# Attention scores of the later chunks: full-width products of stacked K parts, one head at a time

## The chip, the cores and the metric

One core of one Trainium2 chip runs the whole program. The metric is the device time of one execution in microseconds (us), the median of the runs of one measurement; lower is better.

## What is computed

Sliding-window attention with a few sink keys over q, k, v of shape 4 x 8 x 768 x 64 (batch, heads, positions, head size), and behind it a gated feed-forward block on the 3072 resulting rows of 512:

```python
scores = (1 / sqrt(D)) * q @ k.T
keep = (pos < n_sink) | ((0 <= rel) & (rel < window))      # 4 sinks, window 128
a = softmax(where(keep, scores, -1e9))                      # row by row, sum + 1e-9
x = (a @ v).transpose(0, 2, 1, 3).reshape(3072, 512)
out = (x @ w_a * (x @ w_b)) @ w_out                         # d_ff = 1536
```

All inputs are fp32. A product of two fp32 matrices is made from rounded parts: `h` (high, type fp32r) and `l` (the rest), as high*high + high*low + low*high.

## The kernel before, in words

The 24 tiles of 128 query rows are dealt into chunks. The first four tiles (tile 0 of each batch) have a path of their own (`first_tiles`). Then `run` takes the chunks of `CHUNKS` in turn: the feed-forward block (`moe`) of one chunk runs on TensorE, and between its products the attention of the next chunk is slipped in (`between`, a generator that is advanced by some steps at each of 33 places). Chunk 0 (2 tiles) uses `parts_exact`, plain fp32; chunks 1 to 6 (3 tiles each, the last two from two batches) use `parts_split`, and these are the later chunks that the change touches.

`moe` walks over j = 0..11: twelve products for `a` (4 blocks of 128 x 3 rounded pairs, 384 columns wide for three tiles), twelve for `b`, and nine of 512 columns into the outputs `o0`, `o1`, `o2` for the j before. ScalarE copies `a` to `g`, VectorE multiplies by `b`, ScalarE rounds it to `gh`, and GpSimd (j < 10) makes the rest `gl`.

`parts_split` of one chunk works on pairs of heads m = 0..3 (8 heads). `prepare(m)` loads K and q of both heads stacked on 128 partitions (head 2m on 0 to 63, head 2m+1 on 64 to 127), and GpSimd rounds them and makes the rests (`round` L383, `rest` L386): `kh`, `kl`, `qh`, `ql`. `scores(m, i)` for tile i makes six products of 64 partitions and 264 columns (128 keys before, 8 sink columns, 128 own keys), three for each head, on the upper and the lower half of TensorE's rows, into two PSUM banks, `s` for the even head and `av` for the odd one. One such group of six is called a unit below; there are 6 chunks x 4 pairs x 3 tiles = 72. VectorE merges the window (L611), subtracts the mask and takes the row minimum (L612), ScalarE makes the exponentials with their sums (L615), VectorE the reciprocal (L617, L618) for both heads in one instruction, ScalarE scales (L620) and copies the 8 sink columns (L625). Later `transposes(h)` turns the three tiles of one head into bank `t` (L631), VectorE writes them to `pt` (L633), `av(m)` multiplies with v (L642: 64 weight columns for each head, so the two heads use the left and the right half of TensorE's columns; called AV below), `sinks_t` and `sinks_av` (L651, L662) add the sinks.

Each PSUM tag (`s`, `av`, `t`, `a`, `b`, `o0`, `o1`, `o2`) is one bank with one buffer. The pool `io` has 6 buffers for everything that is loaded in this phase. The order of instructions on each engine is fixed when the program is built: the framework's scheduler places them, starting from the order of the code.

Of the kernel before, what the change touches and what calls it, by code (L numbers as in the profile page):

```python
# [19 lines left out]
P = 128  # L20
# [207 lines left out]
class Fast:  # L228
    def __init__(self, tc, ctx, ident, ins, out, chk):
        self.tc, self.nc, self.ident, self.out, self.chk = tc, tc.nc, ident, out, chk  # L230
        self.kT, self.kD, self.qT, self.qP, self.vB, self.vS, self.kq0, self.v0, self.wa, self.wb, self.wo = ins
# [5 lines left out]
        self.at = pool("f_at", 4)  # L237
# [159 lines left out]
    def prep_kq(self, places, m, tag):  # L397
        raws = []
        for b, t0, n, s0, nb, kw, *_ in places:
            kr = self.io([P, 4 * KB - NS], F32, f"kr{tag}_{m}_{b}")  # L400
            self.nc.sync.dma_start(kr[:, :kw], self.kT[b, m, :, s0 * KB:s0 * KB + kw])
            raws.append(kr)
        qr = self.io([P, 3 * P], F32, f"qr{tag}_{m}")
        for b, t0, n, *_, i in places:
            self.nc.sync.dma_start(qr[:, i * P:(i + n) * P], self.qP[b, m, :, t0 * P:(t0 + n) * P])
        kh, kl = (self.sp.tile([P, MK], F32R, tag=k, name=f"{k}{tag}_{m}") for k in ("kh", "kl"))
        qh, ql = (self.sp.tile([P, 3 * P], F32R, tag=k, name=f"{k}{tag}_{m}") for k in ("qh", "ql"))
        for kr, (*_, kw, col, _, _) in zip(raws, places):
            cols = slice(col, col + kw)
            self.round(kh[:, cols], kr[:, :kw])  # L410
            self.rest(kl[:, cols], kr[:, :kw], kh[:, cols])
# [133 lines left out]
    def attention(self, parts, xf, after):  # L545

        prepare, values, sinks, scores, transposes, av, sinks_t, sinks_av = parts
        values(0)
        for k in range(6 * NP + 7):
            m, r = divmod(k, 6)  # L550
            if r == 2 and m:
                transposes(2 * m - 1)
            if r % 2 == 0 and m < NP:
                scores(m, r // 2)
            if r == 0 and m > 1 and m % 2:
                sinks_av(m // 2 - 1, 1, xf)
            if r == 0 and m + 1 < NP:
                prepare(m + 1)
            if r == 1 and m:
                transposes(2 * m - 2)  # L560
            if r == 3 and m and m % 2 == 0:
                sinks_t(m // 2 - 1)
            if r == 4 and m:
                av(m - 1, xf)
                if m < NP:
                    values(m)
# [489 lines left out]
```

## Time and profile before

| | |
|---|---|
| median of 3 runs | 780.69 us (779.58 to 780.88) |
| profiled execution, its own time | 778.73 us |
| span of its instructions | 777.0 us |
| TensorE matmul busy | 766.9 us (99%) |
| VectorE, ScalarE, GpSimd busy | 370.9, 372.2, 191.2 us |
| granted TensorE clock, mean | 0.999 |

The profiled execution is 1.96 us faster than the median of the timed runs; 1.7 us of its time lie outside the span. Matmul records overlap, since a matmul's record reaches from its start to the modelled landing of its result while the next one already streams; so "99% busy" says that TensorE never has nothing under way, and what a matmul costs is read from start to start.

### The profile page before, as it was taken

Reading aid. Unit: us, or ns where it says so; the run is one execution under the profiler, and the core shown is the slowest. Engines: PE = TensorE matmul, PEld = TensorE weight load, DVE = VectorE, ACT = ScalarE, POOL = GpSimd, SP = SyncE. Lnnn points to the kernel's source line nnn. Section 1 sums busy time; section 2 is a strip of 40 time slices with the busy share of each in tenths; the row PEclk is TensorE's granted clock in tenths of the full one; section 3 lists DMA queues with packets and bytes.
Section 4 is the critical chain, followed back from the end, with each engine's and each line's share of the span. In section 5 each row is a group of like instructions: output and inputs, shape, how many; then the busy total and the mean of one; then the engine's idle time right before and its main releaser. Section 6 shows DMA issues by size and latency. Waiting matters only on the chain.

```text
span 777.0 us, 12872 instructions
## 1 busy us (share of the span) xinstructions
PE 766.9 (99%) x4580; PEld 661.9 (85%) x4582; DVE 370.9 (48%) x1161; ACT 372.2 (48%) x1123; POOL 191.2 (25%) x252
## 2 busy tenths in 40 slices
PE   8999999999999999999999999999999999999997
PEld 6887777888888889888888888888888888899996
DVE  6899999345344443345433444334443445221001
ACT  6577755465355553555435554354544555331111
POOL 2300022043214132231413314134241432101110
PEclk9999999999999999999999999999999999999999
DMA  8996101312102142132321223213343130010001
GB/s 336 398 346 222 33 26 27 130 39 77 55 28 80 60 152 93 41 99 67 127 91 62 80 89 118 78 68 100 97 131 99 59 93 19 18 41 1 1 1 43
DMA packets 44261, 72.36 MB, mean 93 GB/s; under 512 B 4576, under 2 KB 24096, under 8 KB 44192
## 3 DMA queue, kind: packets, MB, share of 16 engines
q1 hardware_dynamic: 41024, 65.98, 25.9%
q10 hardware_dynamic: 3168, 5.51, 1.9%
q8 instruction: 37, 0.61, 0.3%
q14 instruction: 32, 0.26, 0.1%
HBM read 65.18 MB, written 6.29 MB: 92 GB/s over the span
## 4 chain that ended last, share of the span: by engine, by line
PE 94%; DMA 2%; DVE 2%; ACT 1%; SPq 0%; issue 0%
PE b L829 27%; PE a L829 26%; PE o L857 26%; PE s L605 5%; PE av L642 4%; PE t L631 2%; DMA kx<-in_kD_dram 1%; DMA v<-in_v_dram 1%; PE s L715 1%; PE sk L662 1%; PE skt L651 1%; PE t L740 0%; PE afirst L829 0%; PE t L752 0%; PE av L605 0%; PE av L506 0%
## 5 line engine op out<-in xcount | busy, mean ns | idle before, releaser
L829 PE MATMUL b<-xh,w_b 128*128 128x384 f32 (+2 forms) x768 | 215.2, 344 | 0.0
L829 PE MATMUL a<-xh,w_a 128*128 128x384 f32 (+2 forms) x760 | 214.5, 346 | 0.0
L857 PE MATMUL o<-w_o,gh 128*128 128x512 f32 x576 | 184.1, 401 | 0.0
L878 POOL TENSOR_TENSOR gl<-g,gh 128x384 fp32r<-128x384 f32 (+1 forms) x70 | 68.1, 973 | 359.0 <-ACT gh L876 358.8
L829 PEld LDWEIGHTS a<-xh,w_a 128*128 128x128 f32 x760 | 137.5, 188 | 11.9 <-ACT p L615 2.1
L829 PEld LDWEIGHTS b<-xh,w_b 128*128 128x128 f32 x768 | 139.4, 188 | 7.6
L829 PE MATMUL b<-xl,w_b 128*128 128x384 f32 (+2 forms) x384 | 130.1, 339 | 0.0
L829 PE MATMUL a<-xl,w_a 128*128 128x384 f32 (+2 forms) x380 | 128.2, 337 | 0.0
L857 PEld LDWEIGHTS o<-w_o,gh 128*128 128x128 f32 x576 | 104.4, 188 | 20.1 <-ACT p L615 1.0
L873 DVE TENSOR_TENSOR g<-b,g 128x384 f32<-128x384 f32 (+2 forms) x96 | 53.4, 557 | 140.2 <-PE b L829 134.8
L857 PE MATMUL o<-w_o,gl 128*128 128x512 f32 x288 | 113.6, 395 | 0.0
L615 ACT ACTIVATE p<-p,st 128x136 f32<-128x136 f32 x144 | 57.7, 402 | 83.2 <-DVE st L612 80.8
L867 ACT COPY g<-a 128x384 f32<-128x384 f32 (+2 forms) x95 | 45.1, 475 | 106.9 <-PE a L829 101.6
L876 ACT CAST gh<-g 128x384 fp32r<-128x384 f32 (+2 forms) x96 | 49.2, 512 | 97.6 <-DVE g L873 96.7
L829 PEld LDWEIGHTS a<-xl,w_a 128*128 128x128 f32 x380 | 71.5, 188 | 3.0
L829 PEld LDWEIGHTS b<-xl,w_b 128*128 128x128 f32 x384 | 72.3, 188 | 1.9
L857 PEld LDWEIGHTS o<-w_o,gl 128*128 128x128 f32 x288 | 54.1, 188 | 13.4 <-DVE gl L878 0.8
L633 DVE TENSOR_TENSOR pt<-t,tri 128x768 f32<-128x768 f32 x48 | 45.8, 955 | 38.1 <-PE t L631 38.1
L611 DVE COPY_PREDICATED s<-own,s 128x128 f32<-128x128 uint16 x72 | 21.1, 293 | 87.4 <-PE av L605 75.7
L620 ACT ACTIVATE p<-p,st 128x136 f32<-128x136 f32 x144 | 51.0, 402 | 23.0 <-DVE st L618 21.0
L617 DVE TENSOR_SCALAR st<-st 128x2 f32<-128x2 f32 x72 | 14.9, 207 | 49.6 <-ACT p L615 49.6
L386 POOL TENSOR_TENSOR kl<-kr,kh 128x536 fp32r<-128x536 f32 (+2 forms) x32 | 36.7, 1146 | 1.8
(174 smaller groups left out, 1046.0 us busy)
## 6 DMA issues: line engine op xcount, KB each, us to landing
raw_a<-in_wa_dram SPq DMA_DIRECT2D x12, 512.0 KB, 7.8
raw_b<-in_wb_dram SPq DMA_DIRECT2D x12, 512.0 KB, 7.3
raw_o<-in_wo_dram SPq DMA_DIRECT2D x12, 512.0 KB, 7.0
chk_a<-in_wa_dram SPq DMA_DIRECT2D x24, 256.0 KB, 3.0
chk_b<-in_wb_dram SPq DMA_DIRECT2D x24, 256.0 KB, 2.9
chk_o<-in_wo_dram SPq DMA_DIRECT2D x24, 256.0 KB, 2.9
out_dram<-os ACTq DMA_DIRECT2D x21, 256.0 KB, 2.1
kr<-in_kT_dram SPq DMA_DIRECT2D x16, 268.0 KB, 2.8
```

The costliest lines, as they stand in the source:

```text
L386: self.nc.gpsimd.tensor_tensor(o, i, high.bitcast(F32), op=ALU.subtract)
L605: nc.tensor.matmul(ss[e], lhsT=q[half[e], cols], rhs=k[half[e], c0:c0 + SW], start=n == 0, stop=n == 2)
L615: nc.scalar.activation(p[:, e], p[:, e], AF.Exp, bias=st[:, 0, e:e + 1], scale=-1.0, accum_out=st[:, 1, e:e + 1])
L620: nc.scalar.mul(p[:, e], p[:, e], st[:, 3, e:e + 1])
L633: nc.vector.tensor_tensor(self.pt_pair()[:, e].rearrange("p (c m) q -> p c m q", m=2), tp.unsqueeze(2).to_broadcast(shape), self.tri.unsqu ...
L642: nc.tensor.matmul(ps[half[e], c * P:(c + ns) * P], lhsT=v[:, e, blk, :], rhs=pt[:, e, sl:sl + ns, :], start=j == 0, stop=j == len(groups) ...
L829: mm = self.nc.tensor.matmul(ps[:, cols], lhsT=w[:, ksl], rhs=x[:, kk, cols], start=start and kk == 0 and i == 0, stop=kk == NK - 1 and i ...
L857: nc.tensor.matmul(outs[i], lhsT=g[:, sl], rhs=w, start=j == 0 and k == 0, stop=j == NJ - 1 and k == 2)
L867: nc.scalar.copy(g[:, :n], pa[:, :n])
L873: nc.vector.tensor_tensor(g[:, :n], pb[:, :n], g[:, :n], op=ALU.mult)
L876: nc.scalar.copy(gh[:, :n], g[:, :n])
L878: e.tensor_tensor(gl[:, :n], g[:, :n], gh[:, :n].bitcast(F32), op=ALU.subtract)
```

## The change

In `parts_split` the heads are taken one at a time. `prepare(h)` loads q of one head twice (partitions 0 to 63 and again 64 to 127; the host lays q out so already) and K of a pair only for even heads. GpSimd writes one tile `ks` of 128 partitions that holds the high part of the head's K on one half and the rest on the other. `scores(h, i)` is then two products over all 128 partitions: `ks` by `qh`, and `ks` by `ql`, into bank `s` alone. The softmax steps are issued for one head. Bank `av` now takes the results of `av` and `sinks_av`. The steps of a chunk are 30 instead of 31, with a new order; `p` and `st` have 6 buffers instead of 4, `v` has 2 instead of 1. AV and the joined key blocks (`groups`) are as before.

```diff
-        self.at = pool("f_at", 4)
+        self.at = pool("f_at", 6)
...
+    def halves(self, h):
+        return (slice(0, D), slice(D, P)) if h % 2 == 0 else (slice(D, P), slice(0, D))
+
+    def prep_kq(self, places, h, tag):
+        if h % 2 == 0:
+            self.kr = []
+            for b, t0, n, s0, nb, kw, *_ in places:
+                kr = self.io([P, 4 * KB - NS], F32, f"kr{tag}_{h}_{b}")
+                self.nc.sync.dma_start(kr[:, :kw], self.kT[b, h // 2, :, s0 * KB:s0 * KB + kw])
+                self.kr.append(kr)
+        qr = self.io([P, 3 * P], F32, f"qr{tag}_{h}")
         for b, t0, n, *_, i in places:
-            self.nc.sync.dma_start(qr[:, i * P:(i + n) * P], self.qP[b, m, :, t0 * P:(t0 + n) * P])
...
+            self.nc.sync.dma_start(qr[:, i * P:(i + n) * P], self.qT[b, h, :, t0 * P:(t0 + n) * P])
+        ks = self.sp.tile([P, MK], F32R, tag="kh", name=f"ks{tag}_{h}")
+        qh, ql = (self.sp.tile([P, 3 * P], F32R, tag=k, name=f"{k}{tag}_{h}") for k in ("qh", "ql"))
+        kh, kl = self.halves(h)
+        for kr, (*_, kw, col, _, _) in zip(self.kr, places):
+            kr = kr[(h % 2) * D:(h % 2 + 1) * D, :kw]
+            self.round(ks[kh, col:col + kw], kr)
+            self.rest(ks[kl, col:col + kw], kr, ks[kh, col:col + kw])
         self.round(qh, qr)
         self.rest(ql, qr, qh)
-        return kh, kl, qh, ql
+        return ks, qh, ql
...
-        v = self.sp.tile([P, 2, MB, D], F32, tag="v", name=f"v{tag}_{m}", bufs=1)
+        v = self.sp.tile([P, 2, MB, D], F32, tag="v", name=f"v{tag}_{m}")
...
+        for h in range(H + 2):
+            for i in range(3):
+                if h < H:
+                    scores(h, i)
+                if i == 0:
+                    if h % 2 == 1 and h > 2:
+                        av(h // 2 - 1, xf)
+                    if h + 1 < H:
+                        prepare(h + 1)
+                    elif h + 1 == H and after:
+                        after[0](0)
+                    if h < H and h % 2 == 0:
+                        values(h // 2)
+                    if h % 4 == 3:
+                        sinks(h // 4)
+                elif h > 4 and h % 4 == 1:
+                    sinks_av(h // 4 - 1, i - 1, xf)
+                if i == 1 and 1 <= h <= H:
+                    transposes(h - 1)
+                if i == 2 and h and h % 4 == 0:
+                    sinks_t(h // 4 - 1)
+                yield
...
+        def scores(h, i):
+            ks, qh, ql = kq[h]
+            u = f"{tag}_{h}_{i}"
+            ps = self.ps.tile([P, SW], F32, tag="s", name=f"s{u}")
+            for n, q in enumerate((qh, ql)):
+                nc.tensor.matmul(ps, lhsT=q[:, i * P:(i + 1) * P], rhs=ks[:, c0s[i]:c0s[i] + SW],
+                                 start=n == 0, stop=n == 1)
+            p = self.at.tile([P, SW], F32, tag="p", name=f"p{u}")[:, :W]
+            st = self.at.tile([P, 4], F32, tag="st", name=f"st{u}")
             mask = self.m1 if tiles[i] == 1 else self.mg
...
-            ps = self.ps.tile([P, nt * P], F32, tag="t", name=f"av{tag}_{m}")
+            ps = self.ps.tile([P, nt * P], F32, tag="av", name=f"av{tag}_{m}")
...
-            ps = self.ps.tile([P, n], F32, tag="t", name=f"sk{tag}_{g}_{pr}")
+            ps = self.ps.tile([P, n], F32, tag="av", name=f"sk{tag}_{g}_{pr}")
...
-                steps = 6 * NP + 7 if c else H * len(nrows) + 5
+                steps = 30 if c else H * len(nrows) + 5
```

The order on TensorE, in the chunk of batch 1 (names begin with its number; the numbers behind are the pair or head, the tile and the buffer), where the AV of the first pair stands. Before, from the last product of `b` of one j to the first of `o`:

```order
L829 MATMUL b_3_2890<-xh,w_b_743 128x384
L605 MATMUL s_1_1_2_2908<-kh_1_1_2645,qh_1_1_2647 128x264
L605 MATMUL av_1_1_2_2909<-kh_1_1_2645,qh_1_1_2647 128x264
L605 MATMUL s_1_1_2_2908<-kl_1_1_2646,qh_1_1_2647 128x264
L605 MATMUL av_1_1_2_2909<-kl_1_1_2646,qh_1_1_2647 128x264
L605 MATMUL s_1_1_2_2908<-kh_1_1_2645,ql_1_1_2648 128x264
L605 MATMUL av_1_1_2_2909<-kh_1_1_2645,ql_1_1_2648 128x264
L642 MATMUL av_1_0_2929<-pt,v_1_0_2617 64x256 x4
L642 MATMUL av_1_0_2929<-pt,v_1_0_2617 64x128 x4
L857 MATMUL o_0_2599<-w_o_765,gh_2_2823 128x512 x2
```

and with the change:

```order
L822 MATMUL a_3_2952<-xh,w_a_698 128x384
L604 MATMUL s_1_3_0_2967<-ks_1_3_2879,qh_1_3_2880 128x264
L604 MATMUL s_1_3_0_2967<-ks_1_3_2879,ql_1_3_2881 128x264
L635 MATMUL av_1_0_2979<-pt,v_1_0_2706 64x256 x4
L635 MATMUL av_1_0_2979<-pt,v_1_0_2706 64x128 x4
L822 MATMUL b_3_3004<-xh,w_b_743 128x384
```

A unit of six half-height products has become a group of two of full height, and AV stands behind such a group.

The place on TensorE where two groups of scores stand closest, at the start of the same chunk. Before, tile 2 of pair 0 stood between `b` and `o`:

```order
L829 MATMUL b_1_2708<-xh,w_b_513 128x384
L605 MATMUL s_1_0_2_2726<-kh_1_0_2393,qh_1_0_2395 128x264
L605 MATMUL av_1_0_2_2727<-kh_1_0_2393,qh_1_0_2395 128x264
L605 MATMUL s_1_0_2_2726<-kl_1_0_2394,qh_1_0_2395 128x264
L605 MATMUL av_1_0_2_2727<-kl_1_0_2394,qh_1_0_2395 128x264
L605 MATMUL s_1_0_2_2726<-kh_1_0_2393,ql_1_0_2396 128x264
L605 MATMUL av_1_0_2_2727<-kh_1_0_2393,ql_1_0_2396 128x264
L857 MATMUL o_0_2599<-w_o_555,gh_0_2667 128x512 x2
```

With the change the groups of head 0, tile 2 and of head 1, tile 0 stand around five products of `a`:

```order
L822 MATMUL a_1_2752<-xh,w_a_487 128x384 x2
L604 MATMUL s_1_0_2_2739<-ks_1_0_2418,qh_1_0_2419 128x264
L604 MATMUL s_1_0_2_2739<-ks_1_0_2418,ql_1_0_2420 128x264
L822 MATMUL a_1_2752<-xl,w_a_487 128x384
L822 MATMUL a_1_2752<-xh,w_a_487 128x384 x2
L822 MATMUL a_1_2752<-xl,w_a_487 128x384
L822 MATMUL a_1_2752<-xh,w_a_487 128x384
L604 MATMUL s_1_1_0_2767<-ks_1_1_2699,qh_1_1_2700 128x264
L604 MATMUL s_1_1_0_2767<-ks_1_1_2699,ql_1_1_2701 128x264
```

Both write bank `s`, so the second group waits until VectorE has read the first; between the two groups ahead of them lie seven products of `a`, and nine or more of `moe` or an AV between any others of this chunk.

The order on GpSimd for the preparation of one pair before:

```order
L383 TENSOR_SCALAR kh_1_3_3003<-kr_1_3_1_2999 128x536
L386 TENSOR_TENSOR kl_1_3_3004<-kr_1_3_1_2999,kh_1_3_3003 128x536
L383 TENSOR_SCALAR qh_1_3_3005<-qr_1_3_3001 128x384
L386 TENSOR_TENSOR ql_1_3_3006<-qr_1_3_3001,qh_1_3_3005 128x384
L878 TENSOR_TENSOR gl_4_3026<-g_4_2975,gh_4_3025 128x384
L878 TENSOR_TENSOR gl_5_3115<-g_5_3091,gh_5_3114 128x384
```

and of two heads now:

```order
L383 TENSOR_SCALAR qh_1_2_2784<-qr_1_2_2781 128x384
L383 TENSOR_SCALAR ks_1_2_2783<-kr_1_2_1_2779 64x536
L386 TENSOR_TENSOR ql_1_2_2785<-qr_1_2_2781,qh_1_2_2784 128x384
L386 TENSOR_TENSOR ks_1_2_2783<-kr_1_2_1_2779,ks_1_2_2783 64x536
L871 TENSOR_TENSOR gl_1_2805<-g_1_2765,gh_1_2804 128x384
L383 TENSOR_SCALAR qh_1_3_2880<-qr_1_3_2877 128x384
L383 TENSOR_SCALAR ks_1_3_2879<-kr_1_2_1_2779 64x536
L386 TENSOR_TENSOR ql_1_3_2881<-qr_1_3_2877,qh_1_3_2880 128x384
L386 TENSOR_TENSOR ks_1_3_2879<-kr_1_2_1_2779,ks_1_3_2879 64x536
L871 TENSOR_TENSOR gl_2_2903<-g_2_2863,gh_2_2902 128x384
```

The four instructions now stand once for each head, with as many columns as before (K on 64 partitions instead of 128), and one `gl` of `moe` between two heads.

## Rows read from the trace of the kernel before

**Rows 1.** The page: busy time of each engine with its share of the span and its instructions, and the chain of work that ended last, by engine.

```profile
PE 766.9 (99%) x4580; PEld 661.9 (85%) x4582; DVE 370.9 (48%) x1161; ACT 372.2 (48%) x1123; POOL 191.2 (25%) x252
...
PE 94%; DMA 2%; DVE 2%; ACT 1%; SPq 0%; issue 0%
```

**Rows 2.** Timeline of PE around one unit between `a` and `b`: start us, duration us, engine, line, operation, tiles, shapes. The odd head's products (`av`) start with the even head's and are left out.

```profile
252.23 0.34 PE L829 MATMUL a<-xh,w_a 128*128 128x384 f32 x1
252.50 0.39 PE L605 MATMUL s<-kh,qh 64*128 64x264 f32 x1
...
252.73 0.28 PE L605 MATMUL s<-kl,qh 64*128 64x264 f32 x1
...
252.85 0.28 PE L605 MATMUL s<-kh,ql 64*128 64x264 f32 x1
...
253.06 0.44 PE L829 MATMUL b<-xh,w_b 128*128 128x384 f32 x1
253.35 0.34 PE L829 MATMUL b<-xl,w_b 128*128 128x384 f32 x1
```

**Rows 3.** Timeline of PE: transposes without a unit behind them (255.28), products of `o`, and transposes with a unit behind them (257.70).

```profile
255.28 0.49 PE L631 MATMUL t<-ident,p 128*128 128x128 f32 x3
255.53 0.70 PE L857 MATMUL o<-w_o,gh 128*128 128x512 f32 x2
256.06 0.40 PE L857 MATMUL o<-w_o,gl 128*128 128x512 f32 x1
256.30 0.63 PE L857 MATMUL o<-w_o,gh 128*128 128x512 f32 x2
...
257.70 0.49 PE L631 MATMUL t<-ident,p 128*128 128x128 f32 x3
258.12 0.38 PE L605 MATMUL s<-kh,qh 64*128 64x264 f32 x1
...
258.68 0.45 PE L829 MATMUL a<-xh,w_a 128*128 128x384 f32 x1
258.96 0.34 PE L829 MATMUL a<-xl,w_a 128*128 128x384 f32 x1
```

**Rows 4.** Timeline of PE: one full-height product of `sinks_av` (L662) between `a` and `b`, then the first and the last of twelve products of `b`, 384 columns each.

```profile
269.57 0.34 PE L829 MATMUL a<-xh,w_a 128*128 128x384 f32 x1
269.75 0.34 PE L662 MATMUL sk<-xh,xl 128*128 128x384 f32 x1
269.93 0.34 PE L829 MATMUL b<-xh,w_b 128*128 128x384 f32 x1
...
271.86 0.34 PE L829 MATMUL b<-xh,w_b 128*128 128x384 f32 x1
```

**Rows 5.** Timeline of PE: the first and the last of twelve products of `a`, 256 columns each, in the feed-forward of the chunk with two tiles.

```profile
172.37 0.28 PE L829 MATMUL a<-xh,w_a 128*128 128x256 f32 x1
...
173.69 0.28 PE L829 MATMUL a<-xh,w_a 128*128 128x256 f32 x1
```

**Rows 6.** Timeline of PE: products of 128 columns, the first and the tenth of a run.

```profile
30.89 0.28 PE L829 MATMUL afirst<-xl,w_a 128*128 128x128 f32 x1
...
31.90 0.28 PE L829 MATMUL afirst<-xl,w_a 128*128 128x128 f32 x1
```

**Rows 7.** Timeline of PE: an AV with no unit ahead of it, between `o` and `a` (256 columns wide).

```profile
208.32 0.40 PE L857 MATMUL o<-w_o,gl 128*128 128x512 f32 x1
208.65 1.52 PE L642 MATMUL av<-pt,v 128*64 128x256 f32 x16
210.10 0.39 PE L829 MATMUL a<-xh,w_a 128*128 128x256 f32 x1
210.33 0.29 PE L829 MATMUL a<-xl,w_a 128*128 128x256 f32 x1
```

**Rows 8.** The full-height scores of chunk 0 (L715), from the answer on that line: the waits that stand ahead of them in the queue of PE (PEldq); duration in ns, min/median/max, first and last start.

```profile
L715 PEldq EVENT_SEMAPHORE  x7: 51/51/51, 31.5 to 102.4; - x7
```

**Rows 9.** Timeline of PE at the last of these waits (102.4).

```profile
102.62 0.40 PE L829 MATMUL b<-xh,w_b 128*128 128x512 f32 x1
...
102.85 0.61 PE L715 MATMUL s<-kx,qx 128*128 128x264 f32 x2
```

**Rows 10.** Timeline of DVE and ACT behind one unit whose last products are in the first row.

```profile
336.32 0.28 PE L605 MATMUL s<-kh,ql 64*128 64x264 f32 x1
...
336.95 0.28 DVE L611 COPY_PREDICATED s<-own,s 128x128 f32<-128x128 uint16 x1
...
337.34 0.29 DVE L612 CUSTOM_DVE_ANT_0 p<-s,mg 128x136 f32<-128x136 f32 x1
...
339.38 0.71 ACT L620 ACTIVATE p<-p,st 128x136 f32<-128x136 f32 x2
```

**Rows 11.** Groups by line, GpSimd, shapes kept apart: count, busy us, mean ns of one, idle time before them and what ended it.

```profile
L878 POOL TENSOR_TENSOR gl<-g,gh 128x384 fp32r<-128x384 f32 x60 | 60.8, 1013 | 324.1 <-ACT gh L876 324.0
L386 POOL TENSOR_TENSOR ql<-qr,qh 128x384 fp32r<-128x384 f32 x24 | 25.0, 1044 | 1.1
L386 POOL TENSOR_TENSOR kl<-kr,kh 128x536 fp32r<-128x536 f32 x16 | 22.2, 1387 | 0.8
L383 POOL TENSOR_SCALAR qh<-qr 128x384 fp32r<-128x384 f32 x24 | 13.1, 546 | 27.4 <-PE av L605 22.6 <-DMA qr<-in_qP_dram 4.6
L383 POOL TENSOR_SCALAR kh<-kr 128x536 fp32r<-128x536 f32 x16 | 10.2, 639 | 28.7 <-DMA kr<-in_kT_dram 17.5 <-issue 11.0
```

More of the change, by code (lines that the diff above doesn't have):

```diff
@@ L547, in attention @@
         prepare, values, sinks, scores, transposes, av, sinks_t, sinks_av = parts
[L548 to L566, printed above, removed]
-                if m % 2:
-                    sinks(m // 2)
-            if r == 5 and m and m % 2 == 0:
-                sinks_av(m // 2 - 1, 0, xf)
-            if r == 5 and m == NP - 1 and after:
-                after[0](0)
-            yield
+        for h in range(H + 2):
[20 more added lines that the diff above has]
+                yield
     def parts_split(self, segs):
@@ L587, in parts_split, with prepare @@
         half = (slice(0, D), slice(D, P))
[L589 to L590 removed]
+        def prepare(h):
+            kq[h] = self.prep_kq(places, h, tag)
         def values(m):
@@ new lines, in scores @@
+        def scores(h, i):
[7 more added lines that the diff above has]
+            st = self.at.tile([P, 4], F32, tag="st", name=f"st{u}")
+            mask = self.m1 if tiles[i] == 1 else self.mg
+            nc.vector.copy_predicated(ps[:, :P], self.own.bitcast(mybir.dt.uint16), ps[:, W:])
+            nc.vector.tensor_tensor_reduce(out=p, in0=ps[:, :W], in1=mask[:, :W], scale=-0.125, scalar=BIG,
+                                           op0=ALU.add, op1=ALU.min, accum_out=st[:, 0:1])
+            nc.scalar.activation(p, p, AF.Exp, bias=st[:, 0:1], scale=-1.0, accum_out=st[:, 1:2])
+            nc.vector.tensor_scalar(st[:, 2:3], st[:, 1:2], 1e-9, None, op0=ALU.add)
+            nc.vector.reciprocal(st[:, 3:4], st[:, 2:3])
+            nc.scalar.mul(p, p, st[:, 3:4])
+            state[h, i] = p
+            if h % 4 == 0:
+                sc[h // 4, i] = self.at.tile([P, 4, NS], F32, tag=f"sc{i}", name=f"sc{u}", bufs=2)
+            nc.scalar.copy(sc[h // 4, i][:, h % 4, :], p[:, P:])
@@ L695, in do_prep @@
             if h % 2 == 0:
-                v = self.sp.tile([P, 2, MB, D], F32, tag="kl", name=f"vx{u}")
+                v = self.sp.tile([P, 2, MB, D], F32, tag="v", name=f"vx{u}")
                 nc.sync.dma_start(v[:, :, :nb], self.vB[b, h // 2, :, :, s0:s0 + nb])
@@ L977, in run, with body @@
         return val, self.ok
-def body(tc, kT, kD, qT, qP, vB, vS, kq0, v0, wa, wb, wo, nw, out):
+def body(tc, kT, kD, qT, vB, vS, kq0, v0, wa, wb, wo, nw, out):
     nc = tc.nc
@@ L988, in body @@
         with ExitStack() as ctx:
-            f = Fast(tc, ctx, ident, (kT, kD, qT, qP, vB, vS, kq0, v0, wa, wb, wo), out, chk)
+            f = Fast(tc, ctx, ident, (kT, kD, qT, vB, vS, kq0, v0, wa, wb, wo), out, chk)
             val, ok = f.run(lambda: scalars_to_float(tc, cp, raw), lambda val, gp: verdict(tc, cp, ident, chk, val, gp))
```

52 lines of the change are left out of this document (4 added, 48 removed).

## The prediction

> **What bounds the kernel now.** First the page: TensorE has work in 99% of the span, every other engine in less than half, and the chain that ended last is TensorE's own for 94% [rows 1]. So the kernel ends when TensorE has streamed everything in its queue, and an edit is worth what it changes between the starts of TensorE's matmuls. The second view is therefore the timeline of PE, read from start to start. A plain product of 384 columns costs 0.1755 us (eleven steps from 269.93 to 271.86, 1.93 us) [rows 4], one of 256 columns 0.120 us (eleven steps from 172.37 to 173.69) [rows 5], one of 512 columns 0.233 us (six steps from 256.30 to 257.70) [rows 3]. Against these a unit of scores can be priced, borders included.
>
> **What a unit costs today.** Between the last product of `a` (252.23) and the second of `b` (253.35) lie 1.12 us [rows 2]; two plain products would take 0.351 us, so the unit costs 0.769 us. It has three parts: 0.27 us from the last `a` to the unit, where 0.1755 is plain (0.095 us of entry); 0.56 us inside; and 0.29 us from the first to the second `b` (0.115 us of exit). The six products run two by two, one on each half of the rows, so the inside holds only three steps. The last two start 0.12 us apart (252.73, 252.85) [rows 2]; the rest is again border. Behind transposes the price is the same: without a unit they cost 0.25 us and the two products behind them 0.53 instead of 0.466 us; with a unit 0.42 us until its start, 0.56 us inside and 0.28 us to the second `a` [rows 3]. The difference is 0.42 + 0.56 + 0.28 - 0.1755 - 0.25 - 0.064 = 0.77 us.
>
> An AV with no unit ahead has an entry of its own: 0.33 us from the last `o` to AV where 0.233 is plain, and 0.23 us behind it where 0.120 is plain [rows 7]. So leaving for work on half the array, and coming back, costs about 0.1 us each way. The order of before puts an AV directly behind the third tile of pairs 1 to 3, that is behind 18 of the 72 units. There the unit has no exit, and AV no entry.
>
> The Trainium skill says as much in "TensorEngine Tiling (Array Packing)", section Key Properties: changing the tiling mode, not just the tile, drains TensorE. The trace agrees, with 0.095 us in and 0.11 us out.
>
> **What the change removes.** 54 units with both borders at 0.769 us are 41.5 us. The 18 ahead of an AV have an entry and 0.56 us, 0.655 us, but their AVs then pay 0.10 us themselves: 18 x 0.555 = 10.0 us. The first unit of all stands in two pieces among the products of `b`, which adds one visit more, 0.77 us. Together 52.3 us.
>
> **What it adds on TensorE.** 6 chunks x 8 heads x 3 tiles x 2 = 288 full-height products of 264 columns. No row shows such a product in fp32r. It is nearest to the 256-column product; 8 columns more at the slope between 256 and 512 columns, (0.233 - 0.120) / 256 us each, give 0.1235 us, and 288 of them 35.6 us. From below, 128 columns still take 0.112 us (nine steps from 30.89 to 31.90 [rows 6]), so less than 32.3 us is excluded; from above, the row of 384 columns would make 50.5 us. I take 0.1235: 264 is next to 256. Borders I take as nothing: the full-height product of `sinks_av` between `a` and `b` starts 0.18 us behind one neighbour and 0.18 us ahead of the next, plain spacing for 384 columns, although its operands come from other engines [rows 4]. A wait of its own in the queue costs nothing either where it is met in time: at 102.4 one stands ahead of a full-height score, which starts 0.23 us behind a 512-column product, as if there were no wait [rows 8, 9].
>
> The sum: 52.3 - 35.6 = 16.7 us less. AV, its column halves, the transposes and the feed-forward keep their counts. The profiled execution would go from 778.73 to 762.0 us; the median stands 1.96 us above that execution, so I predict 780.69 - 16.7 = **764.0 us**.
>
> **What lies beside.** GpSimd prepares each head with the four instructions that served a pair. Their columns are the same, so between half and all of the old time for the K part; I take all: 0.546 + 0.639 + 1.044 + 1.387 = 3.62 us a head [rows 11], and twice the old sum of GpSimd's preparation in all, some 90 us more on 191 [rows 1]. Where does it wait? `ks` has two buffers, so head h+1 may start when tile 2 of head h-1 is through TensorE, and must be done before tile 0 of head h+1. In the new order 36 products of 384 columns, nine of 512, the three transposes and three groups stand between: 6.3 + 2.1 + 0.3 + 3 x 0.25, about 9.5 us, against 3.62 us and one `gl` of 1.01 us [rows 11]. For the two chunks with two batches K has 664 columns instead of 536, at the same rate 4.1 us a head; in one head of each the load of q also waits for a buffer that GpSimd frees in the same preparation, which takes part of what is left. Covered, I think; if that cover were gone, each head that is 1 us late costs 1 us, 48 heads in all.
>
> VectorE's L617 and L618 come twice as often with one column instead of two, and ScalarE's small copy L625 with 8 instead of 16; both engines are at 48% of the span [rows 1], so their sum is no bound, and what counts is lateness. The softmax of one pair took from 336.60 (0.28 us behind the start of its last products) to 340.09, 3.5 us [rows 10]; one head is shorter, and its transposes come behind 21 products and two groups, some 4.7 us. In the queue of VectorE the product with `b` may stand in between (it waits for the end of `b`); that leaves about 1 us.
>
> The tightest is bank `s`, now one buffer for all scores. VectorE lets go of it after L611 and L612: 0.20 us until the next starts and 0.29 us [rows 10], with 0.28 us for the product's own end some 0.8 us after the last product's start. The closest two groups have five products of 384 columns between them, 0.88 us, plus the 0.12 us of the last product itself: 1.0 us. This occurs once a chunk (seven products of 256 columns in chunk 1); elsewhere at least 1.1 us lie there, mostly 2. Where VectorE first has to wait for the exponential of the tile before, such a place can be up to 0.5 us late: at most 6 x 0.5 = 3 us. I take none.
>
> **Rivals.** (A) As above, 764.0 us; its own range, from the 0.112 us floor of a product (3.3 us less) and 3 us of late banks, is 760.7 to 767. Chance 0.79.
>
> (B) Gain given back by the single bank or by late softmax steps. For: `s` and `av` were two banks for one unit, now one bank serves twice as many groups, and transposes come two steps behind their scores instead of three. Against: the distances above. With a mean of 0.05 us at each of 144 groups 7 us are lost: 771 us. It decides only from 0.116 us a group (16.7 / 144). Chance 0.12.
>
> (C) Slower: the borders belong not to half-height work but to any break in the stream of `moe`'s weights behind a wait. Then each of the 144 groups pays 0.20 us, 28.8 us in all, and the time is 764.0 + 28.8 = 792.8 us; from 0.116 us a group it decides. For: nearly every group now begins with a wait on VectorE or GpSimd. Against: the products of `sinks_av` and the scores of chunk 0 pay none [rows 4, 8, 9]. Chance 0.05.
>
> (D) Slower: packing is worth more than I credit. If all borders were slack that something else would fill, only the steps count, three of 0.12 us for four of 0.1235 us: 0.134 us a unit, 9.6 us, 790.3 us. Against: borders are spans in which no matmul starts, on an engine that is never without work. Chance 0.02.
>
> The rule that speaks for D is in the Trainium skill, "TensorE: Matmul & The Clock Gate", Part 3 (Packing small matmuls): products on distinct row groups run concurrently, so small contractions should be packed. The trace agrees in that six products take three steps; but a visit of three steps does not earn its two borders.
>
> (E) Little change, because the span turns out bound elsewhere, 775 to 782 us: chance 0.02; nothing but TensorE is near full.
>
> **How the numbers follow.** The likeliest case gives 764.0. The range of 760.5 to 770 holds nearly all of A and half of B and leaves out C, D and E. Within 0.2% (1.6 us, what a measurement of this kernel can tell from no change) I put 0.02; slower are C and D, 0.07; faster are A and B, 0.91.
>
> **What would show it.** In the profile of the changed kernel: two products a group, 0.12 us apart, with 0.1755 us from the last 384-column product to the group and 0.18 behind its first neighbour (if 0.27 and 0.29, C is right). AV keeps 0.33 and 0.23 at its borders. Gaps on PE that end with VectorE (L610) or ScalarE (L615) show B, above all at the start of each chunk. GpSimd near 280 us busy, and no PE wait that ends with it. TensorE stays at 99% and the chain at 94%.
>
> What would make it wrong: the granted clock falling in a stretch, or a 264-column fp32r product at something far from 0.12 us.

## The result

The changed kernel takes 762.4 us (median of 4 runs, 761.01 to 762.9) against 780.13 us for the kernel before, timed beside it (778.88 to 780.88): a ratio of 0.977, 95% interval 0.975 to 0.979. The gain is 17.7 us where 16.7 us were predicted. The profiled execution has a span of 760.2 us and a time of 761.92 us.

The page of the changed kernel, the same rows as [rows 1]:

```profile
PE 749.6 (99%) x4436; PEld 668.2 (88%) x4438; DVE 396.1 (52%) x1305; ACT 392.8 (52%) x1195; POOL 282.2 (37%) x364
...
PE 94%; DMA 2%; DVE 2%; SPq 0%; ACT 0%; issue 0%; DVEq 0%
```

TensorE has 144 products fewer (432 half-height ones out, 288 full-height ones in), and is still busy in 99% of the span, with 94% of the chain. GpSimd went from 191 to 282 us.

PE's timeline around one group of scores of the changed kernel, which answers to [rows 2]:

```profile
312.74 0.33 PE L822 MATMUL a<-xh,w_a 128*128 128x384 f32 x1
312.91 0.28 PE L604 MATMUL s<-ks,qh 128*128 128x264 f32 x1
313.03 0.28 PE L604 MATMUL s<-ks,ql 128*128 128x264 f32 x1
313.15 0.33 PE L822 MATMUL b<-xh,w_b 128*128 128x384 f32 x1
313.32 0.34 PE L822 MATMUL b<-xl,w_b 128*128 128x384 f32 x1
```

From start to start, 0.17 us lie ahead of the group, 0.12 us between its two products, 0.12 us behind the second, and 0.17 us to the next product of `b`: plain spacing everywhere, no border. A visit of a head costs 0.24 us where a visit of a pair cost 0.769 us.

PE's timeline at one AV of the changed kernel, to be held against [rows 7]:

```profile
259.71 0.28 PE L604 MATMUL s<-ks,ql 128*128 128x264 f32 x1
259.92 1.52 PE L635 MATMUL av<-pt,v 128*64 128x256 f32 x16
261.37 0.73 PE L850 MATMUL o<-w_o,gh 128*128 128x512 f32 x2
261.95 0.39 PE L850 MATMUL o<-w_o,gl 128*128 128x512 f32 x1
```

AV keeps its borders: 0.21 us where 0.12 is plain, and 0.58 us for two products of `o` where 0.46 is plain.

Where the time went is read from starts on TensorE. The feed-forward of the two-tile chunk, beside which the attention of chunk 1 runs, began at 149.21 us before and begins at 151.07 us now, so the first part became 1.86 us longer. From there to the last start on TensorE (the stretch of the later chunks below) the time went from 621.77 to 603.13 us, 18.64 us less. The 16.8 us between the two spans are these two. Neither is what the sum spoke of: the first was not in it, and the second is 2 us too large.

**The first loss** is a group that comes late. VectorE and PE of the changed kernel, at the start of a chunk:

```profile
315.22 0.28 PE L604 MATMUL s<-ks,qh 128*128 128x264 f32 x1
...
315.43 0.56 DVE L866 TENSOR_TENSOR g<-b,g 128x384 f32<-128x384 f32 x1 [0.52 <-PE b L822]
...
315.90 0.28 DVE L609 COPY_PREDICATED s<-own,s 128x128 f32<-128x128 uint16 x1
...
316.22 0.30 DVE L610 CUSTOM_DVE_ANT_0 p<-s,mg 128x136 f32<-128x136 f32 x1
...
316.68 0.35 PE L604 MATMUL s<-ks,qh 128*128 128x264 f32 x1
316.87 0.28 PE L604 MATMUL s<-ks,ql 128*128 128x264 f32 x1
...
317.19 0.29 DVE L609 COPY_PREDICATED s<-own,s 128x128 f32<-128x128 uint16 x1 [0.67 <-PE s L604]
...
317.52 0.30 DVE L610 CUSTOM_DVE_ANT_0 p<-s,mg 128x136 f32<-128x136 f32 x1
...
317.69 0.34 PE L822 MATMUL a<-xh,w_a 128*128 128x384 f32 x1
...
317.97 0.36 PE L604 MATMUL s<-ks,qh 128*128 128x264 f32 x1
318.17 0.29 PE L604 MATMUL s<-ks,ql 128*128 128x264 f32 x1
```

VectorE is in the product with `b` from 315.43 to 315.99, so it reads `s` only from 315.90 to 316.52, and the group at 316.68 starts right behind that. Its two products are 0.19 us apart instead of 0.12. Behind it VectorE reads `s` at once (317.19, the product of 316.87 has just ended), and is through at 317.82; still the next group is 0.28 us behind its neighbour (317.69 to 317.97, plain 0.17), and its products are 0.20 us apart.

A group is called late here when its products stand over 0.18 us apart; its lateness is what the steps ahead of it and inside it exceed the plain ones by. Of the 144 groups 17 are late, by 2.6 us together: seven in chunk 1, and two at the start of each other chunk. In six VectorE has the product with `b` ahead of the reading of `s`, as at 315.43. Seven stand closely behind a late group, as the one at 317.97, and VectorE reads at once. In four, all in chunk 1, VectorE does the product that writes `pt` (0.95 us, as at 178.0) between its two readings of `s`. Each of the 17 starts 0.15 to 0.17 us behind the end of VectorE's second reading of the group ahead, as at 316.68 and 317.97. About half of the 2.6 us lies inside the groups: the product behind a late one is 0.07 to 0.08 us late itself.

None of this stands in the list of PE's waits of the changed kernel, whose five lines are:

```profile
PE av L511 <- DMA kx<-in_kD_dram: 1.7, 1, 1.7
PE warm L311 <- DVE m L262: 1.3, 1, 1.3
PE t L733 <- DVE st L716: 0.7, 1, 0.7
PE t L733 <- DVE ptx L755: 0.7, 1, 0.7
PE xt L527 <- DVE x L521: 0.6, 1, 0.6
```

While a product that started earlier still counts as busy, a late start of 0.1 us is no idle time. Start-to-start spacing shows it, the waits do not.

**The second loss** is the third line of this list, at 118 us, in the part ahead of chunk 1. VectorE and GpSimd of the changed kernel there:

```profile
117.41 1.82 POOL L386 TENSOR_TENSOR ks<-kr,ks 64x536 fp32r<-64x536 f32 x1
118.29 1.49 DVE L871 TENSOR_TENSOR gl<-g,gh 128x512 fp32r<-128x512 f32 x1
119.70 0.28 DVE L762 TENSOR_TENSOR xf<-t,xf 128x128 f32<-128x128 f32 x1
120.04 0.33 PE L733 MATMUL t<-ident,p 128*128 128x128 f32 x1 [0.67 <-DVE st L716]
```

The `gl` takes 1.49 us; the longest of the 26 that VectorE made before the change took 0.69. It ends 0.55 us behind GpSimd's subtraction for the K part of the second head (117.41 + 1.82 = 119.23), which had started first. (That subtraction is slow too, 1.82 us where 1.36 is the mean; it began 0.07 us behind another VectorE step with two inputs in SBUF, L346 at 117.34.) Behind it in VectorE's queue stand the steps for which the transposes of the exact chunk wait (L762 and L716), so TensorE goes on 0.8 us late.

Of the other 1.0 us, 0.2 us are there at 10 us already, from a cause that stays open, and 0.8 us come with a meeting of the same kind at 19 us, in code that the change did not touch. Before the change VectorE started first, after it GpSimd did:

```profile
18.81 0.69 DVE L335 SCALAR_TENSOR_TENSOR wf_b<-raw_b,wf_b 128x512 int32<-128x512 int32 x1
19.09 1.56 POOL L362 TENSOR_TENSOR w_a<-wf_a,w_a 128x512 fp32r<-128x512 f32 x1 [0.73 <-ACT w_a L356]
```

```profile
18.76 1.29 POOL L362 TENSOR_TENSOR w_a<-wf_a,w_a 128x512 fp32r<-128x512 f32 x1 [0.74 <-DVE wf_b L334]
18.80 1.80 DVE L335 SCALAR_TENSOR_TENSOR wf_b<-raw_b,wf_b 128x512 int32<-128x512 int32 x1
```

This is decided by 0.04 us and is no part of the change: of the three experiments with the order and loads of before, `full6` went the first way (VectorE at 19.34, 0.69 us), `full4` and `atfirst` the second (GpSimd at 19.37 and 18.98, VectorE 1.79 and 1.80 us).

**The gain that was not foreseen** lies in the plain products. Before the change, 24 products of 384 columns in a row, up to the first of `o`, and the same of the changed kernel behind it:

```profile
306.93 0.34 PE L829 MATMUL a<-xh,w_a 128*128 128x384 f32 x1
...
311.16 0.63 PE L857 MATMUL o<-w_o,gh 128*128 128x512 f32 x2
```

```profile
302.46 0.34 PE L822 MATMUL a<-xh,w_a 128*128 128x384 f32 x1
...
306.65 0.63 PE L850 MATMUL o<-w_o,gh 128*128 128x512 f32 x2
```

4.23 against 4.19 us, though neither the products nor their order within the run changed. The mean over all steps between neighbouring plain products of the later chunks went from 175.97 to 174.75 ns at 384 columns (1541 and 1546 steps), from 118.8 to 115.5 at 256 (235 and 245) and from 232.4 to 230.6 at 512 (607 and 614). That is 1546 x 1.22 + 245 x 3.4 + 614 x 1.84 ns = 3.8 us. The granted clock is 0.999 in the one and 0.998 in the other, so it is not the clock.

### The profile page after: what moved, and what is told of

The parts are those of the page before. It is cut to its first block, busy times and chain, and to the rows that moved or that the text cites. A ratio compares the mean times of both kernels' runs of the same rounds, so it can differ in the third digit from the quotient of the medians.

```text
span 760.2 us, 13133 instructions
## 1 busy us (share of the span) xinstructions
PE 749.6 (99%) x4436; PEld 668.2 (88%) x4438; DVE 396.1 (52%) x1305; ACT 392.8 (52%) x1195; POOL 282.2 (37%) x364
## 4 chain that ended last, share of the span: by engine, by line
PE 94%; DMA 2%; DVE 2%; SPq 0%; ACT 0%; issue 0%; DVEq 0%
PE b L822 26%; PE a L822 26%; PE o L850 26%; PE s L604 5%; PE av L635 5%; PE t L624 2%; DMA kx<-in_kD_dram 1%; DMA v<-in_v_dram 1%; PE s L708 1%; PE sk L655 1%; PE skt L644 1%; PE t L733 0%; PE afirst L822 0%; PE t L745 0%; DVE wf_a L335 0%
## 5 line engine op out<-in xcount | busy, mean ns | idle before, releaser
L822 PE MATMUL b<-xh,w_b 128*128 128x384 f32 (+2 forms) x768 | 212.9, 341 | 0.0
L822 PE MATMUL a<-xh,w_a 128*128 128x384 f32 (+2 forms) x760 | 212.0, 342 | 0.0
L850 PEld LDWEIGHTS o<-w_o,gh 128*128 128x128 f32 x576 | 103.8, 188 | 18.9 <-issue 1.0
L866 DVE TENSOR_TENSOR g<-b,g 128x384 f32<-128x384 f32 (+2 forms) x96 | 53.4, 556 | 116.0 <-PE b L822 114.8
L612 ACT ACTIVATE p<-p,st 128x136 f32<-128x136 f32 x144 | 58.6, 407 | 71.6 <-DVE st L610 70.3
L609 DVE COPY_PREDICATED s<-own,s 128x128 f32<-128x128 uint16 x144 | 42.0, 292 | 81.9 <-PE s L604 80.5
L615 ACT ACTIVATE p<-p,st 128x136 f32<-128x136 f32 x144 | 58.7, 408 | 37.1 <-DVE st L614 34.5
L386 POOL TENSOR_TENSOR ks<-kr,ks 64x536 fp32r<-64x536 f32 (+1 forms) x64 | 71.6, 1129 | 3.8
L383 POOL TENSOR_SCALAR qh<-qr 128x384 fp32r<-128x384 f32 x48 | 24.9, 519 | 90.0 <-PE s L604 42.8
L613 DVE TENSOR_SCALAR st<-st 128x1 f32<-128x1 f32 x144 | 21.9, 152 | 67.6 <-ACT p L612 67.5
```

The costliest lines, as they stand in the source:

```text
L386: self.nc.gpsimd.tensor_tensor(o, i, high.bitcast(F32), op=ALU.subtract)
L609: nc.vector.copy_predicated(ps[:, :P], self.own.bitcast(mybir.dt.uint16), ps[:, W:])
L612: nc.scalar.activation(p, p, AF.Exp, bias=st[:, 0:1], scale=-1.0, accum_out=st[:, 1:2])
L615: nc.scalar.mul(p, p, st[:, 3:4])
L822: mm = self.nc.tensor.matmul(ps[:, cols], lhsT=w[:, ksl], rhs=x[:, kk, cols], start=start and kk == 0 and i == 0, stop=kk == NK - 1 and i ...
L850: nc.tensor.matmul(outs[i], lhsT=g[:, sl], rhs=w, start=j == 0 and k == 0, stop=j == NJ - 1 and k == 2)
```

## The experiments

All differ from the kernel they name by the lines shown. The theories: (A) of the prediction, a border belongs to half-height work; (B), lateness gives something back; (C), a border belongs to any break; (D), packing saves its steps. And for the plain products: (P) the place of the operands in SBUF, against (Q) the missing half-height work or the new order.

**`half`: the height alone.** From the changed kernel:

```
+            r = half[h % 2]
             for n, q in enumerate((qh, ql)):
-                nc.tensor.matmul(ps, lhsT=q[:, i * P:(i + 1) * P], rhs=ks[:, c0s[i]:c0s[i] + SW],
+                nc.tensor.matmul(ps, lhsT=q[r, i * P:(i + 1) * P], rhs=ks[r, c0s[i]:c0s[i] + SW],
```

> The changed kernel with each group's two score products cut to one half of the rows (64 instead of 128; the other half is left out of the sums); order, banks, waits, columns and counts stay. If the borders belong to half-height work (A): each of the 144 groups gets about 0.095 us ahead and 0.11 us behind, 144 x 0.20 = 28.8 us, so about 791 us against the changed kernel's 762.4; the 18 groups directly ahead of an AV pay only the entry and take 0.1 us off the AV's own, which makes it about 144 x 0.2 - 18 x 0.2 = 25 us, 787. If a border belongs to any break behind a wait (C), the changed kernel pays them already and nothing changes: 762.

Measured: 809.3 us, ratio 1.038 (1.035 to 1.040). That is 46.9 us above the changed kernel, 0.33 us a group: C falls, and A's direction holds, but its size is far off. One group of this kernel on PE:

```profile
331.01 0.34 PE L823 MATMUL b<-xh,w_b 128*128 128x384 f32 x1
331.27 0.39 PE L605 MATMUL s<-ks,qh 64*128 64x264 f32 x1
331.50 0.28 PE L605 MATMUL s<-ks,ql 64*128 64x264 f32 x1
331.71 0.44 PE L823 MATMUL a<-xh,w_a 128*128 128x384 f32 x1
331.99 0.34 PE L823 MATMUL a<-xl,w_a 128*128 128x384 f32 x1
```

0.26 us lie ahead of it where 0.17 is plain, then 0.23 and 0.21 us where 0.12 is plain, then 0.28 us where 0.175 is plain. So there are four extra pieces of about 0.1 us, not two: each change of height costs the product on either side of it. 0.09 + 0.11 + 0.09 + 0.105 makes 0.395 us a visit, or 0.2 us each way. The mean of 0.33 is lower because the 18 groups ahead of an AV pay nothing more on leaving, some 40 ahead of transposes pay less, and all but one of the late groups of the changed kernel are on time here.

**`three`: the price of a product.** From the changed kernel, `for n, q in enumerate((qh, ql, ql))` with the stop at `n == 2`.

> The changed kernel with a third full-height product per group (the one with the rest of q is issued twice, so that its part enters the scores double). Price of one more product of 264 columns: 0.121 us (the step between the two products of a group in the trace of after) x 144 = 17.4 us, so about 780 us, level with the kernel before. If late groups hide it (the second product of a late group stands behind a wait anyway), a little less, 16 us. If TensorE had slack that a product could fill, less than 10 us.

Measured: 777.8 us, ratio 0.997 (0.996 to 0.999), 15.4 us above the changed kernel. In the stretch of the later chunks the trace has 620.11 us against 603.13, so 17.0 us or 0.118 us a product; 0.8 us of that are gained back in the first part, which this edit does not touch. The steps inside its groups are 0.122 us on the mean. A product costs about what its step shows, and TensorE has no slack to hide one.

**`full4` and `full6`: the products alone, in the order of before.** From the kernel before:

```
-            for n, (k, q) in enumerate(((kh, qh), (kl, qh), (kh, ql))):
-                for e in range(2):
-                    nc.tensor.matmul(ss[e], lhsT=q[half[e], cols], rhs=k[half[e], c0:c0 + SW],
-                                     start=n == 0, stop=n == 2)
+            for e in range(2):
+                for n, q in enumerate((qh, ql)):
+                    nc.tensor.matmul(ss[e], lhsT=q[:, cols], rhs=(kh, kl)[n][:, c0:c0 + SW],
+                                     start=n == 0, stop=n == 1)
```

`full6` keeps the three combinations and only takes `q[:, cols]` and `k[:, c0:c0 + SW]` for each bank.

> The kernel before with only its score products changed: per unit four full-height products (two for each of the pair's banks) in place of six half-height ones; the heads are not kept apart in the sums, so the output is not the reference's. Order by pairs, both banks, GpSimd's work, the softmax and the loads of before stay. The sum of the prediction (52.3 us of visits removed, 288 products at now 0.1205 us = 34.7 us added) speaks of TensorE alone, so all of it should be here: 780.1 - 17.6 = 762.5 us. If part of the gain of the change came from the order by heads, 766 to 775. If the plain steps of the feed-forward get shorter as in the changed kernel (174.5 instead of 176 ns for 384 columns) because half-height work is gone, some 4 us more: 758.5; if that comes from something else, 762.5.

> The kernel before with its six score products of a unit at full height instead of half (one after the other, where they ran two by two; the heads are not kept apart in the sums). If a visit costs 0.769 us of which 0.41 us are borders: 432 x 0.1205 = 52.1 us against 52.3 us, so no change, 780 us. If only the steps count, as in rival D (three of 0.12 us become six): 72 x 0.36 = 26 us more, 806 us.

Measured: `full4` 764.8 us, ratio 0.982 (0.979 to 0.984); `full6` 780.55 us, ratio 1.001 (1.000 to 1.002). Twice the matmul steps at full height cost what the packed ones cost with their borders, so D falls: of 0.769 us only 0.36 us were work. `full4` is 14.7 us faster than the kernel before, and 15.4 us in the stretch of the later chunks (606.37 us); the expectation had 17.6. In one place, for which the expectation had no term, GpSimd's `gl` is late, behind its work on K:

```profile
568.77 0.74 POOL L386 TENSOR_TENSOR kl<-kr,kh 128x264 fp32r<-128x264 f32 x1
...
569.48 0.99 POOL L878 TENSOR_TENSOR gl<-g,gh 128x384 fp32r<-128x384 f32 x1
...
570.52 0.51 PE L857 MATMUL o<-w_o,gl 128*128 128x512 f32 x1 [0.92 <-POOL gl L878]
```

(The same place is late by 0.6 and 0.7 us in `full6` and `atfirst`.) With that stretch of 1.1 us set aside it is 16.5 us, so 1.1 us of the expectation stay unaccounted for. Its plain steps are those of before (175.92, 118.9 and 232.7 ns). Half-height scores are gone here, so the first half of Q falls too.

**`banks`: two score banks.** From the changed kernel:

```
-            ps = self.ps.tile([P, SW], F32, tag="s", name=f"s{u}")
+            ps = self.ps.tile([P, SW], F32, tag=("s", "av")[(3 * h + i) % 2], name=f"s{u}")
```

and the tag `t` instead of `av` for the outputs of `av` and `sinks_av`.

> The changed kernel with the score groups alternating between two banks (`s` and `av`), AV and the sinks' products in the transposes' bank `t`, as before the change. 17 of the 144 groups in the trace of after are late, 12 of them at the starts of chunks, by 2.6 us in all. If the single bank does it, about 2.5 us come back: 760 us. If the softmax behind it or the inputs from GpSimd do it, less than 0.5 us come back: 762. If AV and transposes now wait for each other in one bank, some us are lost: 764 to 768.

Measured: 759.0 us, ratio 0.973 (0.972 to 0.975), some 3 us ahead of the changed kernel by the ratios, and no version here is faster. Counted as above, no group is late any more. The edit did one thing more: with a second bank free, the scheduler put two groups near the start of each chunk directly behind each other:

```profile
314.41 0.29 PE L604 MATMUL s<-ks,ql 128*128 128x264 f32 x1
314.54 0.29 PE L604 MATMUL s<-ks,qh 128*128 128x264 f32 x1
...
315.36 0.29 DVE L610 CUSTOM_DVE_ANT_0 p<-s,mg 128x136 f32<-128x136 f32 x1
```

The group at 314.54 starts 0.8 us before VectorE's second reading of the one ahead of it, so at these places bank and order changed together. The four groups of chunk 1 that waited behind the writing of `pt` kept the product ahead of them and are on time as well. With the 0.15 to 0.17 us that all 17 kept to VectorE's readings, it was the bank, and not GpSimd's work on the inputs. In the one trace the later chunks are only 1.5 us shorter (753.04 - 151.41 = 601.63 us): of the 2.6 us, 0.3 go into one set of transposes that now waits for `t`, and 0.3 into plain steps of 174.95 instead of 174.75 ns; the rest is not accounted for.

**`noprep`: GpSimd's cover.** From the changed kernel, `prep_kq` returns the tiles of head h - 2, when there are any, ahead of its four GpSimd steps.

> The changed kernel without GpSimd's preparation for heads 2 to 7 of each chunk (36 of 48 heads; their scores use the rounded K and Q of heads 0 and 1, the loads stay). GpSimd then works some 130 us less. If its work is fully covered, as taken: no change, 762.4 +- 1. If it costs TensorE time, by late `ks` and `ql` or by slowing VectorE where both work at once (one `gl` on VectorE took 1.49 instead of 0.69 us beside GpSimd's work on K), 1 to 5 us come back: 758 to 761.

Measured: 764.8 us, ratio 0.980 (0.978 to 0.982): not faster, and by the medians 2.4 us slower than the changed kernel, although the intervals of the two ratios meet. GpSimd is busy for 150.7 us instead of 282.2, so its sum costs nothing, but the meetings with VectorE moved. At the end of chunks its work on the sinks now coincides with VectorE's `xl` and `gl`:

```profile
493.09 0.73 POOL L386 TENSOR_TENSOR xl<-vsr,xl 64x256 fp32r<-64x256 f32 x1
493.13 1.10 DVE L808 TENSOR_TENSOR xl<-xf,xh 128x384 fp32r<-128x384 f32 x1
...
494.16 0.55 DVE L873 TENSOR_TENSOR gl<-g,gh 128x384 fp32r<-128x384 f32 x1
494.76 0.51 PE L852 MATMUL o<-w_o,gl 128*128 128x512 f32 x1 [0.21 <-DVE gl L873]
```

The `xl` takes 1.10 us where such a step took 0.55 us in the changed kernel, and two products of `o` behind it start 0.65 and 0.61 us after the ones ahead of them, where 0.23 is plain. Of the 24 steps `xl` in the later chunks seven take 0.63 to 1.10 us here, and none over 0.56 us in the changed kernel. Five products of `o` are late by 1.8 us together, and the products behind them by 0.1 us each, 0.8 us more; the stretch of the later chunks is 2.85 us longer. What matters is where GpSimd's work falls, not how much there is.

**`qfirst` and `norest`: the meeting at 118 us.** Both from `banks`, both for head 1 of the first later chunk. `qfirst` puts the steps of Q ahead of K's in the source; `norest` has

```
-            self.rest(ks[kl, col:col + kw], kr, ks[kh, col:col + kw])
+            if tag == self.tag1 and h == 1:
+                self.nc.scalar.copy(ks[kl, col:col + kw], kr)
+            else:
+                self.rest(ks[kl, col:col + kw], kr, ks[kh, col:col + kw])
```

> The kernel with two score banks (banks), in which GpSimd prepares head 1 of the first later chunk in another order: Q ahead of K. In banks as in the changed kernel, GpSimd's subtraction for that head's K starts 0.9 us before VectorE's `gl` (118.3 us), which then takes 1.49 instead of 0.69 us, and TensorE waits 0.7 us. If the two engines get in each other's way there, the wait goes and 0.8 us come back: 758.2 against 759.0 us, and `gl` takes 0.69 us. If `gl` is late for another reason, it stays at 1.49 us. If another step of VectorE now meets GpSimd, some other wait of up to 1 us appears.

> The kernel with two score banks, in which one subtraction of GpSimd's is left out (the rest of K for head 1 of the first later chunk; ScalarE copies K there instead, so that head's scores are wrong). It runs beside VectorE's `gl` at 118 us in every kernel with the new order. If the two get in each other's way, `gl` takes 0.69 us instead of 1.49, TensorE's wait of 0.7 us behind it goes, and 0.8 us come back: 758.2 against 759.0 us (at the edge of what the times tell; the trace decides). If `gl` is slow for a reason of its own, it stays at 1.49 us.

`qfirst` tells nothing: 759.0 us, and in its trace GpSimd still does K first, the program's scheduler put it there again; `gl` took 1.49 us as ever. `norest` took 759.85 us, ratio 0.973 (0.972 to 0.975), which cannot be told from `banks`, but its trace decides:

```profile
118.70 0.69 DVE L874 TENSOR_TENSOR gl<-g,gh 128x512 fp32r<-128x512 f32 x1
119.64 0.20 PEld L736 LDWEIGHTS t<-ident,p 128*128 128x128 f32 x2 [0.31 <-DVE xf L765]
```

Without GpSimd's subtraction `gl` takes 0.69 us, and the transposes come 0.25 us behind its end. They start 0.28 us behind the product ahead of them, in `banks` 1.08 us. So the two engines do get in each other's way, at a price of 0.8 us here.

The Trainium skill explains it in "SBUF — State Buffer", section "SBUF: two separate sides": VectorE and GpSimd share a pair of ports, for which a VectorE operation with two SBUF inputs and a reading GpSimd operation exclude each other for a whole instruction. The traces agree: at 18.8 and at 118 us the later of the two ends 0.55 us behind the end of the earlier.

**`atfirst`, `pad704`, `pad352`: the place.** `atfirst` is the kernel before with `self.at = pool("f_at", 4)` moved ahead of the weights' pool, so that the weights lie higher and `xh`, `xl`, `gh` and `gl` stay. `pad704` is `banks` with

```
+        pool("f_pad", 1).tile([P, 176], F32, name="pad")
         self.mo = pool("f_mo", 2)
```

and `pad352` has 88 instead of 176.

> The kernel before with one pool (the softmax tiles) placed ahead of the weights instead of behind them in SBUF: all other tiles lie some kilobytes higher, nothing else changes. If the plain 384-column step (176.0 ns on average in the trace of before, 174.5 in that of after) depends on where the operands lie, its mean moves by 1 ns or more and the time by 2 us or more. If it depends on what interrupts the stream, it stays at 176.0 and the time at 780.

> The kernel with two score banks (banks) and 704 unused bytes per partition ahead of the last pool, which holds xh, xl, gh and gl: they then lie exactly where they lay before the change (the pools ahead of it had shrunk by 704 bytes in the change); the instructions stay. If the shorter plain steps of the changed kernel come from the distance between these tiles and the weights, the steps go back: 384 columns 174.9 to 176.0 ns, 256 columns 115.4 to 118.8, 512 columns 230.6 to 232.5, some 1540 x 1.1 + 245 x 3.4 + 615 x 1.9 ns = 3.7 us on the stretches counted, about 4 us with the rest: 763 against 759.0 us. If they come from the order or from the missing half-height products: 759.0.

> As pad704, with half of it, 352 bytes: a distance that neither kernel has. If the plain step depends on the distance, its mean for 384 columns may be any of the levels seen so far (174.5 to 176.0 ns), and the time follows it between 757 and 764 us. If it doesn't, 174.9 ns and 759.0 us.

Measured: `atfirst` 776.3 us, ratio 0.996 (0.995 to 0.998), without any edit to the work. `pad704` 762.9 us, ratio 0.978 (0.977 to 0.980), 3.9 us above `banks`; `pad352` 760.6 us, ratio 0.975 (0.973 to 0.977). The mean plain steps, worked out as above from the starts of neighbouring products (the last column is the median of the kernel; the kernel before, timed beside each, took 779.4 to 780.5 us):

| kernel | 384 columns, ns | 256 | 512 | us |
|---|---|---|---|---|
| before | 175.97 | 118.8 | 232.4 | 780.1 |
| `full4` | 175.92 | 118.9 | 232.7 | 764.8 |
| `atfirst` | 174.46 | 119.4 | 230.9 | 776.3 |
| after | 174.75 | 115.5 | 230.6 | 762.4 |
| `banks` | 174.95 | 115.4 | 230.6 | 759.0 |
| `pad704` | 175.91 | 119.0 | 232.8 | 762.9 |
| `pad352` | 174.38 | 117.0 | 232.6 | 760.6 |

In `pad704` the 24 products take 4.22 us again:

```profile
303.11 0.34 PE L823 MATMUL a<-xh,w_a 128*128 128x384 f32 x1
...
307.33 0.63 PE L851 MATMUL o<-w_o,gh 128*128 128x512 f32 x2
```

704 unused bytes bring all three steps back to those of before, with the order and the products of `banks`. So P holds: the pools ahead of `xh` and `gh` had shrunk by 704 bytes with the change (`kl` gone, a second buffer for `v`, two more for the softmax tiles), and that alone was worth 3.9 us by the medians, 3.4 us by the stretch of the later chunks in the two traces. The other traces agree: the seven with the pools of the changed kernel (`half`, `three`, `noprep`, `qfirst` and `norest` among them) have 174.5 to 175.1, 115.0 to 116.0 and 230.0 to 230.6 ns, the four with the pools of before (`full6` among them) 175.9 to 176.0, 118.8 to 119.0 and 232.4 to 232.8 ns. Why one place is better than another stays open, and so does whether the distance counts or the place itself. `pad352` shows that the three widths do not move together: its 512 columns are as slow as before the change, its 384 columns about as fast as after it.

## Why the prediction was right, point by point

**The bound** held: TensorE 99%, chain 94%, and the edits that add or take away products on it (`half`, `three`, `full4`) move the time by about what their starts move.

**The visit of 0.769 us** held as a sum; `full6` shows it directly. Its division was wrong: "about 0.1 us each way" was half of what leaving costs. The prediction saw 0.27 us ahead and 0.29 us behind, and put the excess inside down as "again border" without adding it to the price. The sum was safe because it took whole visits, but the same price was then used for what a break would cost (rival C) and in the expectation of `half`, which came out at 47 us where 25 to 29 stood.

**The product** was taken at 0.1235 us and costs 0.120 to 0.122 by its step, 0.118 in `three`: at 0.1205 us 288 of them are 34.7 us, not 35.6. **The missing borders** were right in every group that is on time.

**GpSimd** was near 280 us as foreseen, with no late `ks` or `ql` in the list of PE's waits, and none behind a late group. That half the partitions cost the full price was right as well:

```profile
L386 POOL TENSOR_TENSOR ks<-kr,ks 64x536 fp32r<-64x536 f32 x32 | 43.5, 1359 | 2.5
L383 POOL TENSOR_SCALAR ks<-kr 64x536 fp32r<-64x536 f32 x32 | 20.4, 637 | 4.5 <-PE s L708 3.3
```

1359 and 637 ns stand where 128 partitions took 1387 and 639 [rows 11]. What failed is "Covered, I think": the cover was reckoned as time on GpSimd, and the price appeared on VectorE, 0.8 us.

**The single bank** was named as the tightest place, with up to 3 us, and then taken as none. It cost 2.6 us. Two steps failed. The bank was to be free some 0.8 us after the start of the last product, within the 1.0 us of the closest place; it took 0.95 us (316.87 to 317.82), and 0.15 us more until the next group began, so that place is 0.1 us late even where VectorE reads at once. The second of VectorE's two readings starts 0.33 us behind the first, where 0.20 was taken from rows of two heads in turn [rows 10]. And the wait was sought in the exponential, at one place in each of six chunks; it was in VectorE's queue, with the product with `b` or the writing of `pt` ahead of a reading, and 17 groups were late. B was real, at a sixth of what it needed to decide.

**Not in the sum at all** was the place of the operands, -3.9 us. The products at their measured price give 52.3 - 34.7 = 17.6 us of gain, the late groups -2.6, the place +3.9 (3.8 by its steps): 18.9 us, where the later chunks show 18.64. Less 0.8 us for `gl`, and 1.0 us for the meeting at 19 us, which falls either way, and the start, 17.0 us are left, and the spans differ by 16.8. The main term was right, shown by `half`, `full4` and `full6`. That the forecast met the time within 1.6 us was also luck: the terms that it left out, -2.6, +3.9 and -1.8 us, nearly cancel.

## What to carry over

A stream of full-height matmuls that is left for a few half-height products pays at four products, here 0.4 us a visit. Packing six products into three steps saved 0.36 us and so earned nothing (`full6`), and stacking them into four full-height products was better (`full4`). So price a visit whole, from the last product ahead of it to the second behind it, and then undo it alone. After a change in the sizes of pools, look at the plain steps before crediting the edit: tiles that moved can be worth as much as a term of the sum. An engine with much spare time can still be dear where its operation coincides with one of VectorE's that somebody waits for.

## What the runs showed of the hardware

A change between half and full height costs about 0.2 us, spread over the product ahead of it and the product behind it (`half`: 0.09 and 0.11 us on entering, 0.09 and 0.105 us on leaving).

The step of a plain matmul depends on where its operands lie in SBUF: between `banks`, `pad352` and `pad704` it goes from 174.4 to 175.9 ns at 384 columns, from 115.4 to 119.0 at 256 and from 230.6 to 232.8 at 512, with instructions and order on TensorE unchanged and a granted clock of 0.998 or 0.999.

A GpSimd operation and a VectorE operation with two SBUF inputs run one behind the other, and the one that started second pays: 1.80 and 1.49 us on VectorE instead of 0.69 (18.80 and 118.29 in the changed kernel), 1.56 us on GpSimd instead of 1.29 (19.09 in the kernel before).

Behind a product that started late after a wait the next step was longer too: 0.19 to 0.20 us instead of 0.12 in the 17 late groups of the changed kernel, and 0.34 us instead of 0.23 behind the late products of `o` (`full4`, `full6`, `noprep`).
